# Modulation columns from column chunks of w_mod, summed by TensorE between V's steps

## The chip, the cores and the metric

The kernel runs on one core of one Trainium2 chip. The metric is the device time of one execution in microseconds (us). A core has five engines that run side by side, each working through its own list of instructions in order: TensorE (PE in the profile, with its weight loads shown apart as PEld), VectorE (DVE), ScalarE (ACT), GpSimd (POOL) and SyncE (SP), which here issues the DMAs. [...]

## The reference, cut to what matters

```python
S, D, H = 2048, 448, 16
mod = (silu(c) @ w_mod).reshape(1, 6, 1, D)          # w_mod: 448 x 2688
sa, ca, ga, sb, cb, gb = (mod[:, i] for i in range(6))
h = layernorm(x) * (1 + ca) + sa                     # x: 1 x 2048 x 448
x = x + ga * attention(h)                            # q, k, v = h @ wqkv, 16 heads, softmax, @ wo
h = layernorm(x) * (1 + cb) + sb
x = x + gb * gated_mlp(h)                            # gelu(h @ w_in), a 2048 x 2048 spatial mix, @ w_out
```

Everything is float32. The change lies in the first line and the first use of it: the vectors `sa` and `ca`, and the first h.

## The kernel before, in words

**Stages.** The kernel starts with a short stage that loads x and weights, normalizes and transposes x and computes V, Q and K; attention over 16 heads follows, then the gated MLP. The change touches the start alone, some 50 of 1402 us. There x is worked on in four groups of 512 rows (`g`), each of four tiles of 128 rows. A group's tile is normalized by VectorE (`ln_stat`, `ln_norm`: statistics, then `xn`), transposed by TensorE into four PSUM banks, one for each 128 columns of D (`tp`, c = 0 to 3, the last with 64 real columns), scaled by `1 + ca` and shifted by `sa` (columns, one value to a partition), and split into a high and a low float32r part, `hT`, since products are made of float32r pieces: high by high, high by low, low by high. The weights are split the same way (`wv` for V, `wqk` for Q and K). `STEPS` lists 11 pairs (piece of h, piece of weight); one unit of V (128 rows) or of Q/K (128 features of one group) is 11 products summed in a PSUM bank. Piece 6 holds column block 3, its high part on partitions 0 to 63 and its low part on 64 to 127; the last two pairs, (6,6) and (6,7), read both.

**The modulation before.** `w_mod` is laid out as four row blocks (k) of 112 rows; `load_mod(0)` reads the 896 columns of `sa` and `ca` in four DMAs, one for each k. VectorE multiplies block k by `silu[:, k]` and adds it up over k in `acc` (`mod_acc`, and `mod_last` for the last k, cut into 128-column pieces). A product of TensorE with a column of ones sums over the 112 partitions and turns the row into a column (`pc`, line 380); `mod_cols` copies it to `col_ca` and `col_sa`. Each float32 product stands as two instructions in the trace, each float32r product and each transpose as one.

**The order.** The schedule is written by hand: each engine runs its instructions as the code issues them. PE starts with products whose results nobody reads (`pe_fill`, tile `wu`), which keep it busy until the transposes of group 0 can be made (`tp_first`). Then `mod_last` (line 364 on), `mod_cols`, `h_hi` (ACT: high part of h straight out of PSUM, line 398), `h_full` (DVE: full h, line 393), `h_lo` (full minus high) and `wv_hi`/`wv_lo` follow for each c; `v_mm` makes V of the first four tiles step by step, then `qk_unit((0, 3), 0)` the first Q/K units, `ln_next(1)` transposes group 1, and `qk_unit((1,), 0)` and `qk_unit((2,), 0)` follow. In `ln_transpose` ACT writes the full h (`hfull`, two buffers, line 125) and its high part (line 132), DVE the low part (line 85, the helper `sub`).

**The queues.** SP issues the loads in the order of the code. A DMA's issue can wait for the one eight places before it, and for the buffer it writes: the first Q/K weights ("a", 128x512 pieces) use the buffers of `wm`, the second ("b") those of V's raw weights.

Of the kernel before, what the change touches and what calls it, by code (L numbers as in the profile page):

```python
# [33 lines left out]
def tile_adaln_mha_gmlp(ctx, tc, x, wqkv, wo, w_in, w_spT, b_sp, w_out, cT, w_mod, out):  # L34
# [136 lines left out]
    def load_mod(pair, eng):  # L171
        for k in range(4):
            wms[pair, k] = e1.tile([112, 2, D], F32, name="wm", tag=("wm", "wm", "raw")[pair], bufs=4)
            eng.dma_start(wms[pair, k], w_mod[:, pair, k])
# [44 lines left out]
    def pe_fill(n, with_):  # L219
        for _ in range(n):  # L220
            pe.matmul(wu[:, 0:128], with_[:, 0:128], ones, start=True, stop=True)
# [25 lines left out]
    def ln_stat(g, ts):  # L247
        if g not in mv1:
            mv1[g] = e1.tile([128, 4, 2], F32, name="mv"), e1.tile([128, 4], F32, name="rs")
        for t in ts:  # L250
            st = e1.tile([128, 6], F32, name="st", bufs=4)
            dve.bn_stats(out=st, in_=xts[4 * g + t])
            dve.bn_aggr(out=mv1[g][0][:, t, :], in_=st)

    def ln_rs(g, a, e):
        mv, rs = mv1[g]
        rstd_of(mv[:, a:e, 1], rs[:, a:e], e - a)

    def ln_norm(g, ts):
        mv, rs = mv1[g]  # L260
        for t in ts:
            xn = e1.tile([128, 512], F32, name="xn", bufs=4)
            dve.tensor_scalar(
                out=xn[:, :D],
                in0=xts.pop(4 * g + t),
                scalar1=mv[:, t, 0:1],
                scalar2=rs[:, t : t + 1],
                op0=ALU.subtract,
                op1=ALU.mult,
            )  # L270
            act.activation(xn[:, D:], xn[:, 384:D], AF.Copy)
            xn1.setdefault(g, []).append(xn)

    def v_mm(kts, steps=STEPS, own=None, kind=None):
        pvs = [ps_o.tile([128, 512], F32, name="pv", tag="o") if kt == own else bank("pv", kind) for kt in kts]
        for j, (a, b) in enumerate(steps):
            for kt, pv in zip(kts, pvs):
                g, t = divmod(kt, 4)
                pe.matmul(pv[:, :D], hT[g][:, a, t * 128 : (t + 1) * 128], wv[:, b, :], start=j == 0, stop=j == NST - 1)  # L279
        return list(zip(kts, pvs))  # L280
# [57 lines left out]
    def tp_first(t):  # L338
        for c in range(4):
            pe.transpose(tps[c][:, t * 128 : (t + 1) * 128], xn1[0][t][:, c * 128 : (c + 1) * 128], ident)  # L340

    x1, x3 = xts[1], xts[3]
    ln_stat(0, (0, 1))
    ln_rs(0, 0, 2)
    ln_norm(0, (0, 1))
    ln_stat(0, (2, 3))
    ln_rs(0, 2, 4)
    mod_acc(0, 0)
    mod_acc(0, 1)
    ln_norm(0, (2, 3))  # L350
    mod_acc(0, 2)
    pe_fill(9, x1)
    tp_first(0)
    tp_first(1)
    pe_fill(5, x3)
    tp_first(2)
    tp_first(3)
    pe_fill(4, x3)

    acc0 = [stage.tile([128, 512], F32, name="acc0", tag="qh")[0:112] for _ in range(2)]  # L360
    wm3 = wms.pop((0, 3))

    def mod_last(c):

# [12 lines left out]
        if c == 3:
            pcs[c] = bank("pc", "s")
        for i, part in enumerate((1, 0)):
            pe.matmul(  # L380
                pcs[c][:, i : i + 1], acc0[part][:, c * 128 : (c + 1) * 128], ones[:112, 0:1], start=True, stop=True
            )

    def mod_cols(c):
        for i, (nm, plus1) in enumerate((("ca", 1.0), ("sa", 0.0))):
# [19 lines left out]
        else:  # L405
            sub(eng, hT[0][64:128, 6, :], fs[3][64:128], hT[0][64:128, 6, :])

    for i in (0, 2, 1, 3):
        load_w("a", i, sp)
    wv_hi(0)  # L410
    wv_hi(2)
    mod_last(0)
    pe_fill(1, x3)
    mod_last(2)
    pe_fill(1, x3)
    mod_last(1)
    pe_fill(1, x3)
    mod_cols(0)
    h_hi(0)
    mod_last(3)  # L420
    mod_cols(2)
    h_hi(2)
    mod_cols(1)
    mod_cols(3)
    wv_hi(1)
    h_hi(1)
    wv_hi(3)
    h_hi(3)
    wv_lo(0, dve)
    wv_lo(2, dve)  # L430
    h_full(0)
    h_lo(0, pool)
    h_full(2)
    h_full(1)
    h_full(3)
    wv_lo(3, pool)
    wv_lo(1, dve)
    h_lo(2, dve)
    h_lo(1, dve)
    h_lo(3, dve)  # L440
    load_x(2, sp)
    for i in (0, 2, 1, 3):
        load_w("b", i, sp)
    pvs = v_mm((0, 1, 3, 2), [STEPS[j] for j in (0, 1, 2, 3, 6, 4, 7, 5, 8, 9, 10)], 3, "s")
    qk_part("a", 0, dve)
    qk_part("a", 2, dve)
    ln_stat(1, (0, 1))
    ln_rs(1, 0, 2)
    ln_stat(1, (2, 3))
    ln_norm(1, (0, 1))  # L450
    ln_rs(1, 2, 4)
    qk_part("a", 1, dve)
    qk_part("a", 3, dve)
    load_mod(1, sp)
    for a in pvs:
        v_copy(*a)
    ln_norm(1, (2, 3))
    load_x(3, sp)
    ln_stat(2, range(4))
    turn[0] = 5  # L460
    qk_unit((0, 3), 0)
    ln_rs(2, 0, 4)

    def ln_next(g):
# [6 lines left out]
            ln_norm(g + 1, range(4))  # L471

    ln_next(1)
    qk_unit((1,), 0)
    qk_unit((2,), 0)
    for i in (0, 2, 1, 3):
        qk_part("b", i, dve)
# [892 lines left out]
```

## Time and profile before

| | |
|---|---|
| time, median of 3 runs | 1404.16 us (1404.03 to 1404.17) |
| the profiled execution | 1404.07 us; its span 1401.8 us |
| PE busy in the span | 1390.6 us (99%) |
| DVE, ACT, POOL busy | 1023.5, 769.9, 288.9 us |
| first product of V (line 279) | at 17.70 us |
| first product of Q/K (line 294) | at 27.11 us |
| first transpose of group 1, of group 2 (line 118) | at 33.51, at 44.75 us |

The span runs from the first to the last instruction; 2.3 us of the execution's time lie around it. Times in the text are counted from the span's start. In a row of the timeline the numbers are the start and the length of a run of equal instructions; in a row of the chain of waits the start and the time that the step holds the chain; in a group's row the busy time, the mean of one instruction, the idle time of the engine ahead of it and what ended that.

### The profile page before, as it was taken

Reading aid. Unit: us, or ns where it says so; the run is one execution under the profiler, and the core shown is the slowest. Engines: PE = TensorE matmul, PEld = TensorE weight load, DVE = VectorE, ACT = ScalarE, POOL = GpSimd, SP = SyncE. Lnnn points to the kernel's source line nnn. Section 1 sums busy time; section 2 is a strip of 40 time slices with the busy share of each in tenths; the row PEclk is TensorE's granted clock in tenths of the full one; section 3 lists DMA queues with packets and bytes.
Section 4 is the critical chain, followed back from the end, with each engine's and each line's share of the span. In section 5 each row is a group of like instructions: output and inputs, shape, how many; then the busy total and the mean of one; then the engine's idle time right before and its main releaser. Section 6 shows DMA issues by size and latency. Waiting matters only on the chain.

```text
span 1401.8 us, 20142 instructions
## 1 busy us (share of the span) xinstructions
PE 1390.6 (99%) x7180; PEld 989.5 (71%) x7180; DVE 1023.5 (73%) x1758; ACT 769.9 (55%) x1477; POOL 288.9 (21%) x275
## 2 busy tenths in 40 slices
PE   7999999999999999999999999999999999999998
PEld 7888655555555555555555555988998888888888
DVE  7778888888888888888888860751357655767474
ACT  3723577766667777777666679263234543434211
POOL 2033312222214143313211231100142330000000
PEclk9999999999999999999999999999999999999999
DMA  8564635555555556654434211534103333446453
GB/s 247 166 178 153 193 103 178 167 161 146 166 159 174 156 165 174 186 145 157 129 94 113 63 50 44 188 115 138 54 0 107 112 113 113 142 136 206 144 170 113
DMA packets 102285, 193.42 MB, mean 138 GB/s; under 512 B 17063, under 2 KB 32039, under 8 KB 99639
## 3 DMA queue, kind: packets, MB, share of 16 engines
q1 hardware_dynamic: 99754, 188.30, 44.3%
q10 hardware_dynamic: 2430, 3.84, 0.7%
q8 instruction: 56, 0.92, 0.3%
q14 instruction: 45, 0.36, 0.1%
HBM read 133.63 MB, written 53.67 MB: 134 GB/s over the span
## 4 chain that ended last, share of the span: by engine, by line
PE 98%; DVE 1%; DMA 1%; SPq 0%; issue 0%; ACT 0%; DVEq 0%; ACTq 0%
PE st_ps L581 18%; PE o_ps L596 17%; PE mt L551 17%; PE acc L1148 6%; PE acc L1150 6%; PE acc L1149 6%; PE z_ps L1074 5%; PE z_ps L960 5%; PE pq L294 5%; PE wo_ps L830 3%; PE pv L279 2%; PE y_ps L1250 2%; PE y_ps L1251 2%; PE y_ps L1249 2%; PE tp L118 1%; DMA wm<-in_w_mod_dram 1%
## 5 line engine op out<-in xcount | busy, mean ns | idle before, releaser
L556 DVE TENSOR_REDUCE pm<-mt 128x1 f32<-128x512 f32 x1024 | 631.4, 682 | 84.1 <-PE mt L551 83.5
L585 ACT ACTIVATE P<-st_ps 128x512 f32<-128x512 f32 x1024 | 514.4, 633 | 205.1 <-PE st_ps L581 205.1
L581 PE MATMUL st_ps<-qst,kst 128*128 128x512 f32 x1024 | 404.2, 406 | 0.2 <-DVE qf L300 0.2
L551 PE MATMUL mt<-kst,qst 128*128 128x512 f32 x1024 | 402.9, 393 | 0.1
L581 PEld LDWEIGHTS st_ps<-qst,kst 128*128 128x128 f32 x1024 | 191.3, 188 | 138.0 <-issue 93.9
L596 PE MATMUL o_ps<-P,V 128*32 128x512 f32 x2048 | 247.1, 598 | 0.0
L551 PEld LDWEIGHTS mt<-kst,qst 128*128 128x128 f32 x1024 | 192.4, 188 | 36.2 <-DVE pm L556 3.7
L724 POOL TENSOR_TENSOR ws_raw<-ws_raw 128x512 f32<-128x512 f32 x80 | 102.9, 1287 | 353.1 <-DMA ws_raw<-in_w_spT_dram 352.9
L1036 ACT ACTIVATE wsp_h<-raw_sp 128x512 fp32r<-128x512 f32 x112 | 70.2, 632 | 162.8 <-PE acc L1150 119.0
L85 DVE TENSOR_TENSOR wsp_l<-raw_sp,wsp_h 128x512 fp32r<-128x512 f32 x112 | 80.6, 730 | 90.5 <-ACT wsp_h L1036 89.6
L596 PEld LDWEIGHTS o_ps<-P,V 128*32 128x32 f32 x2048 | 54.7, 109 | 123.0 <-issue 114.7
L1148 PE MATMUL acc<-wsp_h,heapA 128*128 128x512 f32 x224 | 87.3, 390 | 0.0
L1149 PE MATMUL acc<-wsp_l,heapA 128*128 128x512 f32 x224 | 87.2, 389 | 0.0
L1150 PE MATMUL acc<-wsp_h,heapA 128*128 128x512 f32 x224 | 87.2, 389 | 0.0
L1149 PE MATMUL acc<-wsp_l,heapB 128*128 128x512 f32 x174 | 67.7, 389 | 0.0
L1150 PE MATMUL acc<-wsp_h,heapB 128*128 128x512 f32 x174 | 67.7, 389 | 0.0
L1148 PE MATMUL acc<-wsp_h,heapB 128*128 128x512 f32 x174 | 67.7, 389 | 0.0
L294 PE MATMUL pq<-heapD,heapD 128*128 128x512 f32 x196 | 62.6, 392 | 0.8 <-ACT heapD L96 0.8
L1078 DVE BATCH_NORM_STATS2 stz<-z 128x6 f32<-128x448 f32 x32 | 19.9, 625 | 50.4 <-ACT z L1077 29.9
L1148 PEld LDWEIGHTS acc<-wsp_h,heapA 128*128 128x128 f32 x224 | 42.0, 188 | 8.9 <-DVE cD L1154 0.3
L1150 PEld LDWEIGHTS acc<-wsp_h,heapA 128*128 128x128 f32 x224 | 42.0, 188 | 8.8
L1149 PEld LDWEIGHTS acc<-wsp_l,heapA 128*128 128x128 f32 x224 | 42.0, 188 | 8.6
(208 smaller groups left out, 1589.7 us busy)
## 6 DMA issues: line engine op xcount, KB each, us to landing
ws_raw<-in_w_spT_dram SPq DMA_DIRECT2D x160, 256.0 KB
ws_scr<-ws_raw SPq DMA_DIRECT2D x80, 256.0 KB
raw_sp<-ws_scr SPq DMA_DIRECT2D x80, 256.0 KB
kst<-qk_scr SPq DMA_DIRECT2D x45, 224.0 KB
qst<-qk_scr SPq DMA_DIRECT2D x45, 224.0 KB
raw_sp<-in_w_spT_dram SPq DMA_DIRECT2D x32, 256.0 KB
qk_scr<-qh SPq DMA_DIRECT2D x28, 256.0 KB
qk_scr<-ql SPq DMA_DIRECT2D x28, 256.0 KB
```

Of the source, the lines that this page charges most:

```text
L85: eng.tensor_tensor(out=dst, in0=a, in1=hi.bitcast(F32), op=ALU.subtract)
L294: pe.matmul(pq, wqk[:, b, m * 128 : (m + 1) * 128], hT[g][:, a, :], start=j == 0, stop=j == NST - 1)
L551: pe.matmul(mt, qst[h % 3][:, t * 128 : (t + 1) * 128], kst[h % 3][:, kb * 512 : (kb + 1) * 512], start=True, stop=True)
L556: dve.tensor_reduce(out=pms[h][:, t, kb : kb + 1], in_=mt, axis=AX.X, op=ALU.max)
L581: pe.matmul(st, kst[h % 3][:, kt * 128 : (kt + 1) * 128], qst[h % 3][:, qb * 512 : (qb + 1) * 512], start=True, stop=True)
L585: act.activation(p, st, AF.Exp, scale=SCALE)
L596: pe.matmul(otile[h][32 * qb : 32 * qb + 32, :], V[:, kt, h, :], ptiles.pop((u, qb)), start=kt == 0, stop=kt == NT - 1)
L724: pool.tensor_tensor(out=a, in0=a, in1=b, op=SUMS[i // 16][2])
L1036: act.activation(hi, raw, AF.Copy)
L1148: pe.matmul(acc[i], zh, hi, start=st == 0, stop=False)
L1149: pe.matmul(acc[i], zh, lo, start=False, stop=False)
L1150: pe.matmul(acc[i], zl, hi, start=False, stop=st == 7)
```

## The change

- The 896 columns for `ca` and `sa` are read in four chunks by columns, each with all four k (`load_mod_chunk`: 448 KB for c = 0, 1, 2, 224 KB for c = 3), in turn with V's weights, in the order 0, 2, 1, 3. The host lays `w_mod` out so that each chunk is contiguous for a partition.
- `mod_acc`, `mod_last` and their VectorE instructions go for this pair. `mod_sum` makes the columns by TensorE alone: chunk c is the stationary operand, `silu[:, k]` the moving one, four products summed over k in PSUM for each of `ca` and `sa` (for c = 3 twice, 64 columns each, to fill both halves of the partitions).
- `mod_sum(0)` stands ahead of the transposes, `mod_sum(2)` behind them, `mod_sum(1)` and `mod_sum(3)` inside V's products, ahead of the fifth and the seventh step, with the work that needs them (`first_cols`). V's steps are put in the order (0,0) (0,3) (3,0) (2,2) (2,5) (5,2) (1,1) (1,4) (4,1) (6,6) (6,7).
- The filling products: 22 with the identity (there from 1.3 us on), 8 with x, 2 between the transposes, in place of 9, 5, 4 and 3 with x.
- `qk_unit((1,), 0)` moves ahead of the transposes of group 1; V's tiles 4 and 5 are made side by side; group 1's statistics come behind all four Q/K weight parts, its second half's `ln_norm` behind the first Q/K units; x's groups 1 and 2 and the Q/K weights are issued in another order.

```diff
+    def load_mod_chunk(c, eng):
+        n = 128 if c < 3 else 64
+        wms[0, c] = e1.tile([112, 1024], F32, name="wm", tag="wm", bufs=4)[:, : 8 * n].rearrange("p (k a n) -> p k a n", a=2, n=n)
+        eng.dma_start(wms[0, c], w_mod[:, c * 1024 : c * 1024 + 8 * n].rearrange("p (k a n) -> p k a n", a=2, n=n))
...
-    load_mod(0, sp)
     for i in (0, 2, 1, 3):
+        load_mod_chunk(i, sp)
         load_w("v", i, sp)
-    load_x(1, sp)
...
+    def mod_sum(c, kind):
+        if c not in pcs:
+            pcs[c] = bank("pc", kind)
+        w = wms.pop((0, c))
         for i, part in enumerate((1, 0)):
-            pe.matmul(
-                pcs[c][:, i : i + 1], acc0[part][:, c * 128 : (c + 1) * 128], ones[:112, 0:1], start=True, stop=True
-            )
+            for r in (0,) if c < 3 else (0, 64):
+                for k in range(4):
+                    pe.matmul(
+                        pcs[c][r : r + w.shape[-1], i : i + 1], w[:, k, part, :], silu[:, k : k + 1], start=k == 0, stop=k == 3
+                    )
...
+    load_w("a", 0, sp)
+    load_w("a", 2, sp)
+    load_x(1, sp)
+    load_w("a", 1, sp)
+    load_w("a", 3, sp)
+    load_x(2, sp)
+
+    ln_stat(0, (0, 1))
+    ln_rs(0, 0, 2)
+    ln_stat(0, (2, 3))
+    ln_rs(0, 2, 4)
+    ln_norm(0, (0, 1))
+    ln_norm(0, (2, 3))
+    pe_fill(22, ident)
+    pe_fill(8, x1)
+    mod_sum(0, None)
+    tp_first(0)
+    tp_first(1)
+    pe_fill(2, x3)
+    tp_first(2)
+    tp_first(3)
+    mod_sum(2, None)
...
+    def first_cols(c):
+        mod_sum(c, "m")
+        wv_hi(c)
+        mod_cols(c)
+        h_hi(c)
+        h_full(c)
+        wv_lo(c, dve)
+        h_lo(c, dve)
+        if c == 3:
+            for i in (0, 2):
+                qk_part("a", i, dve)
+
+    pvs = v_mm(
+        (0, 1, 3, 2),
+        [STEPS[j] for j in (0, 2, 4, 1, 3, 5, 6, 7, 8, 9, 10)],
+        3,
+        "s",
+        {4: lambda: first_cols(1), 6: lambda: first_cols(3)},
+    )
...
+    turn[0] = 5
+    qk_unit((0, 3), 0)
     ln_norm(1, (2, 3))
     load_x(3, sp)
+    qk_unit((1,), 0)
     ln_stat(2, range(4))
-    turn[0] = 5
-    qk_unit((0, 3), 0)
     ln_rs(2, 0, 4)
...
-        v_tile(4 * g)
-        v_tile(4 * g + 1)
+        if g == 1:
+            for a in v_mm((4, 5)):
+                v_copy(*a)
+        else:
+            v_tile(4 * g)
+            v_tile(4 * g + 1)
```

TensorE's list of instructions from the program's start to V's last product. Before, filling products (`wu`), the transposes (`tp`) and, after VectorE's sums (`acc`), two products with ones for each c (`pc`), then V's 44 products (`pv`) in one piece:

```order
L221 MATMUL wu<-ones,xg 128x128 x9
L340 MATMUL tp<-ident,xn 128x128 x8
L221 MATMUL wu<-ones,xg 128x128 x5
L340 MATMUL tp<-ident,xn 128x128 x8
L221 MATMUL wu<-ones,xg 128x128 x4
L380 MATMUL pc<-ones,acc_227 128x1
L380 MATMUL pc<-ones,acc_226 128x1
```

The same place in the changed program:

```order
L226 MATMUL wu<-ones,ident 128x128 x22
L226 MATMUL wu<-ones,xg 128x128 x8
L358 MATMUL pc<-silu,wm 128x1 x8
L347 MATMUL tp<-ident,xn 128x128 x8
L226 MATMUL wu<-ones,xg 128x128 x2
L347 MATMUL tp<-ident,xn 128x128 x8
L358 MATMUL pc<-silu,wm 128x1 x8
L286 MATMUL pv<-wv,heapD_89 128x448 x16
L358 MATMUL pc<-silu,wm 128x1 x8
L286 MATMUL pv<-wv,heapD_89 128x448 x8
L358 MATMUL pc<-silu,wm 64x1 x16
L286 MATMUL pv<-wv,heapD_89 128x448 x20
```

Eight products with ones (16 instructions) have become 40 products with `silu` (80 instructions), 24 of them inside V's.

VectorE's list around the last of the columns and the splits of h (`heapD_89` from `hfull`), of V's weights (`wv`) and of the Q/K weights (`heapD_91`, `heapF` from `raw`). Before:

```order
L386 TENSOR_SCALAR col_ca<-pc 128x1
L386 TENSOR_SCALAR col_sa<-pc 128x1
L85 TENSOR_TENSOR wv<-raw,wv 128x448 x2
L393 TENSOR_SCALAR hfull<-tp,col_ca,col_sa 128x512 x4
L85 TENSOR_TENSOR wv<-raw,wv 128x448
L85 TENSOR_TENSOR heapD_89<-hfull,heapD_89 128x512 x2
L85 TENSOR_TENSOR heapD_89<-hfull,heapD_89 64x512
L85 TENSOR_TENSOR heapD_91<-raw,heapD_91 128x512
```

In the changed program, for c = 3, the last in turn:

```order
L364 TENSOR_SCALAR col_ca<-pc 128x1
L364 TENSOR_SCALAR col_sa<-pc 128x1
L371 TENSOR_SCALAR hfull<-tp,col_ca,col_sa 128x512
L85 TENSOR_TENSOR wv<-raw,wv 64x448
L85 TENSOR_TENSOR heapD_89<-hfull,heapD_89 64x512
L85 TENSOR_TENSOR heapD_91<-raw,heapD_91 128x512
L85 TENSOR_TENSOR heapF<-raw,heapD_91 128x512 x2
L85 TENSOR_TENSOR heapF<-raw,heapF 64x512
L257 BN_STATS st<-xg 128x6
```

The splits that the last steps of V need, and the four of the Q/K weights, now stand behind columns that TensorE makes in the middle of V; and the two subtractions that POOL did (c = 0's `h_lo`, c = 3's `wv_lo`) are VectorE's. Both readers of a bank `tp` are ordered: `h_full(c)` waits for `h_hi(c)`.

More of the change, by code (lines that the diff above doesn't have):

```diff
@@ L173, in load_mod @@
             wms[pair, k] = e1.tile([112, 2, D], F32, name="wm", tag=("wm", "wm", "raw")[pair], bufs=4)
-            eng.dma_start(wms[pair, k], w_mod[:, pair, k])
+            a = (pair * 4 + k) * 2 * D
+            eng.dma_start(wms[pair, k], w_mod[:, a : a + 2 * D].rearrange("p (a b) -> p a b", b=D))
+    def load_mod_chunk(c, eng):
+        n = 128 if c < 3 else 64
+        wms[0, c] = e1.tile([112, 1024], F32, name="wm", tag="wm", bufs=4)[:, : 8 * n].rearrange("p (k a n) -> p k a n", a=2, n=n)
+        eng.dma_start(wms[0, c], w_mod[:, c * 1024 : c * 1024 + 8 * n].rearrange("p (k a n) -> p k a n", a=2, n=n))
     def load_x(g, eng):
@@ L272, in ln_norm, with v_mm @@
             xn1.setdefault(g, []).append(xn)
-    def v_mm(kts, steps=STEPS, own=None, kind=None):
+    def v_mm(kts, steps=STEPS, own=None, kind=None, mid=None):
         pvs = [ps_o.tile([128, 512], F32, name="pv", tag="o") if kt == own else bank("pv", kind) for kt in kts]
         for j, (a, b) in enumerate(steps):
+            if mid and j in mid:
+                mid[j]()
             for kt, pv in zip(kts, pvs):
@@ L406, in h_lo @@
             sub(eng, hT[0][64:128, 6, :], fs[3][64:128], hT[0][64:128, 6, :])
-    for i in (0, 2, 1, 3):
-        load_w("a", i, sp)
-    wv_hi(0)
[L411 to L417, printed above, removed]
+    load_w("a", 0, sp)
[19 more added lines that the diff above has]
+    mod_sum(2, None)
+    wv_hi(0)
     mod_cols(0)
     h_hi(0)
-    mod_last(3)
+    wv_lo(0, dve)
+    h_full(0)
     mod_cols(2)
+    h_lo(0, dve)
+    wv_hi(2)
     h_hi(2)
[L423 to L429, printed above, removed]
-    wv_lo(2, dve)
[L431 to L437, printed above, removed]
-    h_lo(2, dve)
-    h_lo(1, dve)
-    h_lo(3, dve)
-    load_x(2, sp)
+    h_full(2)
+    wv_lo(2, dve)
+    h_lo(2, dve)
+    def first_cols(c):
[16 more added lines that the diff above has]
+    )
+    for i in (1, 3):
+        qk_part("a", i, dve)
     for i in (0, 2, 1, 3):
         load_w("b", i, sp)
-    pvs = v_mm((0, 1, 3, 2), [STEPS[j] for j in (0, 1, 2, 3, 6, 4, 7, 5, 8, 9, 10)], 3, "s")
-    qk_part("a", 0, dve)
-    qk_part("a", 2, dve)
+    load_mod(1, sp)
+    for a in pvs:
+        v_copy(*a)
     ln_stat(1, (0, 1))
@@ L473, in tile_adaln_mha_gmlp @@
     ln_next(1)
-    qk_unit((1,), 0)
     qk_unit((2,), 0)
@@ L507, in tile_adaln_mha_gmlp @@
             load_head(0, 1536, S)
-        v_tile(4 * g)
-        v_tile(4 * g + 1)
+        if g == 1:
+            for a in v_mm((4, 5)):
+                v_copy(*a)
+        else:
+            v_tile(4 * g)
+            v_tile(4 * g + 1)
         if g == 3:
@@ L1345 @@
     from concourse.bass_utils import run_bass_kernel_spmd as _run
+    wm = _np.asarray(inputs["w_mod"]).reshape(4, 112, 3, 2, 448).transpose(1, 2, 0, 3, 4)
+    w_mod = _np.concatenate(
+        [wm[:, 0, :, :, c : c + 128].reshape(112, -1) for c in (0, 128, 256, 384)] + [wm[:, 1:].reshape(112, -1)], axis=1
+    )
     lay = {
@@ L1355 @@
         "cT": inputs["c"].reshape(4, 112).T,
-        "w_mod": _np.asarray(inputs["w_mod"]).reshape(4, 112, 3, 2, 448).transpose(1, 2, 0, 3, 4),
+        "w_mod": w_mod,
     }
```

38 lines of the change are left out of this document (removed).

## The prediction

> **What bounds the kernel now.** I read the page first, then PE's waits, then the chain of waits and the timeline of the first 70 us.
>
> ```profile
> PE 98%; DVE 1%; DMA 1%; SPq 0%; issue 0%; ACT 0%; DVEq 0%; ACTq 0%
> PE wu L221 <- DVE st L252: 4.9, 1, 4.9
> PE tp L340 <- DVE xn L263: 1.3, 1, 1.3
> PE pq L294 <- ACT heapD L96: 0.8, 1, 0.8
> PE st_ps L581 <- DVE qf L300: 0.2, 1, 0.2
> ```
>
> PE is the chain for 98% of the span, and the four rows of its waits are all: after the Q/K wait at 31 us it stands still for 0.2 us in 1370. So whatever moves PE's list at some 50 us moves the end by as much; nothing later can take it up. The question is when PE ends group 2's transposes (46.42 us), behind which both programs list the same products: 44 of V, 44 of Q/K, 32 transposes and 22 more of V stand ahead of that in each.
>
> ```profile
> 4.94 4.18 PE L221 MATMUL wu<-ones,xg 128*128 128x128 f32 x18 [4.94 <-DVE st L252]
> 8.91 1.91 PE L340 MATMUL tp<-ident,xn 128*128 128x128 f32 x8
> 10.62 1.39 PE L221 MATMUL wu<-ones,xg 128*128 128x128 f32 x10
> 17.70 9.57 PE L279 MATMUL pv<-wv,heapD 128*128 128x448 f32 x44
> 27.11 1.52 PE L294 MATMUL pq<-heapD,heapD 128*128 128x512 f32 x6
> 33.51 1.91 PE L118 MATMUL tp<-ident,xn 128*128 128x128 f32 x16
> 44.75 1.91 PE L118 MATMUL tp<-ident,xn 128*128 128x128 f32 x16
> 46.42 4.73 PE L279 MATMUL pv<-wv,heapD 128*128 128x448 f32 x22
> ```
>
> ```profile
> 14.42 0.89 PE wu L221 x8
> 15.83 0.33 PE wu L221 x2
> ...
> 17.50 0.35 PE pc L380 x4
> ...
> 33.67 1.75 PE tp L118 x16
> 35.41 5.02 PE pq L294 x22
> 40.43 4.48 PE pv L279 x22
> ```
>
> The chain gives PE's price for one instruction with no wait in it: 0.204 us for V (4.48/22), 0.228 for Q/K (5.02/22), 0.109 for a transpose, 0.111 for a filling one (0.89/8). By these V's 44 need 8.96 us, while the starts 17.70 and 27.11 leave 9.41: 0.45 of waits. The first 22 of Q/K need 5.0 and have 6.40 (27.11 to 33.51): 1.4 of waits. Those 1.85 us and an earlier start of V are all that there is to win.
>
> **Price of a column sum.** Twelve `pc` instructions and six filling ones lie between 15.83 and 17.85 (17.50 + 0.35): 2.02/18 = 0.112 us each, so a product of one column costs as much as one of 128; its weight load sets the pace. For 64 columns:
>
> ```profile
> 65.21 0.94 PE L237 MATMUL pc<-ones,acc 112*128 112x1 f32 x10
> 66.08 2.51 PE L279 MATMUL pv<-wv,heapD 128*128 128x448 f32 x11
> ```
>
> The ten (six of 128 columns, four of 64) take 0.87 until V goes on; less 6 x 0.112 that leaves 0.05 for each of 64. Eight float32 products are 16 instructions, so `mod_sum` of c = 0, 1, 2 costs 16 x 0.112 = 1.8 us, that of c = 3 32 x 0.05 = 1.6. Bounds: 0.112 for 64 columns too (3.6), and below nothing but the product itself.
>
> **Start of V.** PE can begin when the identity is made, at 1.3.
>
> ```profile
> 1.00 0.29 POOL masks.py:199 TENSOR_SCALAR_AFFINE_SELECT ident<-ident 128x128 f32<-128x128 f32 x1
> 8.63 0.63 DVE L252 BATCH_NORM_STATS2 st<-xg 128x6 f32<-128x448 f32 x1 [0.66 <-DMA xg<-in_x_dram]
> 11.69 1.15 DVE L232 SCALAR_TENSOR_TENSOR acc<-wm,silu,acc 112x896 f32<-112x896 f32 x1 [0.90 <-DMA wm<-in_w_mod_dram]
> 12.76 0.93 DVE L263 TENSOR_SCALAR xn<-xg,mv,rs 128x448 f32<-128x448 f32 x2
> ```
>
> PE starts slow: the first 18 products take 4.18/18 = 0.232 us, the transposes behind them 0.24; only within the next ten, at about 10.8, does the price fall to 0.11. That is 5.9 us after the first. Counted from 1.35 the fast clock comes at 7.2, and 25 of the 60 filling instructions are slow; the other 35 end at 7.2 + 35 x 0.111 = 11.1. Then `mod_sum(0)` 1.8, eight transposes 0.87, four fillings 0.44, eight transposes 0.87, `mod_sum(2)` 1.8: V starts at 16.9, **0.8 earlier** than 17.70. The covers hold: x's last piece lands at 8.6 and w_mod's second DMA at 11.6 (392 KB each, two in 3.0 us), so the 448 KB of chunk 0 are there at 10.3 and, behind V's 224 KB, chunk 2 at 13; the last two `xn`, behind L232's 1.15 us before, end no later than the 13.7 of before, and PE asks for them at 14.2. VectorE's sums of w_mod go, but they win only what PE's own list ahead of V lets through.
>
> [...]
>
> The rows give these bounds: no earlier than chunk 0 (V at 16.1), no later than a fast clock at 10.8 as before (12.9 for the fillings, V at 18.7).
>
> **Inside V.** 8.96 for V, 1.8 and 1.6 for the sums: 12.4 us. And a new wait. The sum of c = 3 ends after 24 products of V, at 16.9 + 4.9 + 3.4 = 25.2. Steps (6,6) and (6,7) need `h_lo(3)`, and between stand in a row:
>
> ```profile
> L386 DVE TENSOR_SCALAR col_ca<-pc 128x1 f32<-128x1 f32 x4 | 0.6, 154 | 0.4 <-PE pc L380 0.4
> L398 ACT ACTIVATE heapD<-tp,col_sa,col_ca 128x512 fp32r<-128x512 f32 x4 | 3.0, 769 | 0.0
> L393 DVE TENSOR_SCALAR hfull<-tp,col_ca,col_sa 128x512 f32<-128x512 f32 x4 | 3.0, 803 | 0.0
> L85 DVE TENSOR_TENSOR wv<-raw,wv 128x448 fp32r<-128x448 f32 x3 | 2.1, 712 | 0.0
> L85 DVE TENSOR_TENSOR heapD<-hfull,heapD 64x512 fp32r<-64x512 f32 x4 | 2.8, 690 | 2.0 <-ACT heapD L132 1.9
> L380 PE MATMUL pc<-ones,acc 112*128 112x1 f32 x16 | 2.2, 237 | 0.0
> ```
>
> 0.2 until the sum is out, 0.25 for the two columns, 0.77 `h_hi`, 0.8 `h_full`, 0.6 `wv_lo`, 0.7 `h_lo`: 3.3 us, to 28.55. PE has three steps between (12 x 0.204 = 2.4, to 27.65) and waits 0.9. V ends at 28.55 + 1.63 = 30.2, 3.1 later than 27.11.
>
> **Behind V.** The first Q/K units run without a wait: chunk 3 frees the buffer of the last "a" weight at 25.2, and such a DMA of 256 KB needs 1.2 us behind another (20.80 to 21.98 below), so it is there before VectorE, whose four low parts (0.65 each, from 28.6) end at 31.2; the first step that reads the third is due at 33. So 5.0 instead of 6.4: they end at 35.2, 1.7 later than 33.51. But now VectorE comes late with everything behind:
>
> ```profile
> 20.80 0.63 ACT L96 ACTIVATE heapD<-raw 128x512 fp32r<-128x512 f32 x1 [0.37 <-DMA raw<-in_wqkv_dram]
> 21.98 0.63 ACT L96 ACTIVATE heapD<-raw 128x512 fp32r<-128x512 f32 x1 [0.54 <-DMA raw<-in_wqkv_dram]
> ...
> L252 DVE BATCH_NORM_STATS2 st<-xg 128x6 f32<-128x448 f32 x16 | 9.6, 603 | 0.9 <-DMA xg<-in_x_dram 0.9
> L253 DVE BATCH_NORM_AGGREGATE mv<-st 128x2 f32<-128x6 f32 x16 | 2.9, 182 | 0.5
> L263 DVE TENSOR_SCALAR xn<-xg,mv,rs 128x448 f32<-128x448 f32 x16 | 7.3, 507 | 1.2 <-POOL rs L109 1.2
> L85 DVE TENSOR_TENSOR heapD<-hfull,heapD 128x512 fp32r<-128x512 f32 x11 | 7.3, 684 | 4.8 <-ACT heapD L132 4.8
> L309 ACT ACTIVATE qh<-pq 128x512 fp32r<-128x512 f32 x10 | 5.6, 596 | 7.9 <-PE pq L294 7.9
> L125 ACT ACTIVATE hfull<-tp,col_sa,col_ca 128x512 f32<-128x512 f32 x12 | 9.2, 771 | 1.5 <-DVE heapD L85 1.5
> L132 ACT ACTIVATE heapD<-hfull 128x512 fp32r<-128x512 f32 x12 | 7.6, 632 | 0.4
> ```
>
> - Group 1's transposes. From 31.2: statistics of four tiles 4 x 0.785 = 3.1, two `xn` 0.9, to 35.2; the two Q/K splits wait for ACT's `qh` (36.0) and end at 37.3; two more `xn` at 37.8 and 38.2. PE ends `qk_unit(1)` at 37.7 and needs the fourth `xn` after three transposes, at 38.0: it waits **0.3**, then 39.8.
> - V of tiles 4 and 5. PE ends `qk_unit(2)` at 42.3. VectorE has split unit 1 by 39.8, does group 2's statistics until 42.9, then the low parts of c = 0 and 2 (44.2). ACT's third `hfull` waits for one of two buffers, freed at 43.6: then 0.77 and 0.63 for each of c = 1 and 3, their low parts at 45.8 and 47.2. V's steps, two products each, reach (1,1) at 44.8 (wait 0.3) and (6,6) at 46.4 (wait 0.8, and some 0.1 for each restart): **1.3** in all, end 48.1.
> - Group 2's transposes. Four `xn` from 47.2 on, the last at 49.0; PE gets to it at 48.4: **0.7**, end 50.5.
>
> **The sum**, against 46.42: start -0.8; sums in V +3.4; V's waits 0.9 for 0.45, +0.45; Q/K's -1.4; then +0.3, +1.3, +0.7. That is +3.95, and 50.5 - 46.42 = 4.1 by the times; I take 4.0. The profiled execution took 1404.07 (2.3 around its span), 0.09 below the median, so the forecast is **1408.1 us**. With the clock's bounds, +3.2 to +5.8. With c = 3 at 3.6, +6.0. If none of the four new waits comes (0.9 + 0.3 + 1.3 + 0.7 = 3.2), +0.8.
>
> **Rivals.**
> 1. VectorE keeps up and the new waits stay out. For it: VectorE had idle time there before (the 1.9 and 4.8 us of its `heapD` rows). Against: its list of 3 us behind h_lo(3) and two subtractions more, which POOL did. +0.8 to +2.7: 1405 to 1406.8.
> 2. The other side: **weight loads vanish behind other products**, and the column sums cost next to nothing. V would start when `h_hi(0)` is ready (transposes over at 14.0, then 0.8: 14.9, 2.0 earlier) and hold no 3.4: 4.0 - 5.4 = -1.4, 1402.7; without the new waits 1399.5. It decides below half of the price: the four sums come to 7.0 us, and at 3.0 the change breaks even. Against it stand the 0.87 us at 65.21, taken between V's products. [...]
> 3. The fillings with the identity don't bring the fast clock earlier than 10.8: +5.8, 1409.9. Against: it came 5.9 us after the first product.
> 4. A sum by TensorE alone that still waits for VectorE: excluded, its operands are DMAs' data and `silu`, which VectorE makes ahead of its first statistics.
>
> **How the numbers follow.** Forecast 0.64, rival 1 0.19, rival 2 0.09, rival 3 0.08. A measurement tells 0.2%, 2.8 us, from no change. Slower by more: the forecast but for early clocks with a missing wait, and rival 3: 0.70. Within: rival 1, half of rival 2, the rest: 0.25. Faster: 0.05. The range, 1405.0 to 1409.3, holds the forecast and rival 1 and leaves out rival 2, rival 3 and the dearest c = 3.
>
> **What would show it.** In the changed profile: V's first product at 16 to 17.5, Q/K's first at 30, group 1's transposes at 37.7, group 2's over at 50.5; PE waits for VectorE in V's last eight products, at line 118 and in tiles 4 and 5; 16 `pc` instructions in 1.8 us. A first Q/K product before 28 would make it wrong (sums cheap, or h_lo(3) early), and so would PE without waits from 36 to 50.

## The result: 0.5% slower, and the place where the time was lost

| | before | after |
|---|---|---|
| median of six runs each, us | 1404.1 (1403.64 to 1404.28) | 1411.44 (1411.01 to 1412.21) |
| the profiled execution, us | 1404.07, span 1401.8 | 1411.14, span 1409.1 |
| V's first product on TensorE, us | 17.70 | 15.62 |
| group 2's transposes over, us | 46.42 | 53.28 |

The ratio of the times is 1.0053, with an interval of 1.004 to 1.0066. The forecast was 1408.1 with a range up to 1409.3: the direction came out, the size did not.

Of the profile after, first the shares of the chain that ended last, by engine, from the page:

```profile
PE 98%; DVE 1%; DMA 0%; ACT 0%; issue 0%; POOL 0%; POOLq 0%; DVEq 0%; ACTq 0%
```

TensorE is the chain as before. All but the last of its waits, 0.2 us, again lie in the first 55 us (engine, line, what it waited for; us in total, times, the longest):

```profile
PE pv L286 <- DVE heapD L85: 2.5, 3, 1.2
PE pv L286 <- ACT heapD L132: 2.1, 3, 1.5
PE wu L226 <- POOL ident masks.py:199: 1.3, 1, 1.3
PE st_ps L580 <- DVE qf L307: 0.2, 1, 0.2
```

The wait of 4.9 us for x's first statistics has gone with the products of the identity, and the waits of the first transposes and of Q/K have gone too. New are 4.6 us at line 286, which is V. The timeline of TensorE says where in V (start, length, line, what, how many):

```profile
1.34 7.02 PE L226 MATMUL wu<-ones,ident 128*128 128x128 f32 x44 [1.34 <-POOL ident masks.py:199]
...
15.62 3.51 PE L286 MATMUL pv<-wv,heapD 128*128 128x448 f32 x16
18.97 1.84 PE L358 MATMUL pc<-silu,wm 112*128 112x1 f32 x16
20.67 1.86 PE L286 MATMUL pv<-wv,heapD 128*128 128x448 f32 x8
22.47 1.41 PE L358 MATMUL pc<-silu,wm 112*64 112x1 f32 x32
23.80 2.72 PE L286 MATMUL pv<-wv,heapD 128*128 128x448 f32 x12
27.24 1.87 PE L286 MATMUL pv<-wv,heapD 128*128 128x448 f32 x8 [0.72 <-DVE heapD L85]
28.95 1.52 PE L301 MATMUL pq<-heapD,heapD 128*128 128x512 f32 x6
...
36.44 1.94 PE L118 MATMUL tp<-ident,xn 128*128 128x128 f32 x16
...
42.41 0.98 PE L286 MATMUL pv<-wv,heapD 128*128 128x448 f32 x2 [1.51 <-ACT heapD L132]
...
46.43 1.27 PE L286 MATMUL pv<-wv,heapD 128*128 128x448 f32 x4 [1.19 <-DVE heapD L85]
...
50.88 2.54 PE L118 MATMUL tp<-ident,xn 128*128 128x128 f32 x16
53.28 4.75 PE L286 MATMUL pv<-wv,heapD 128*128 128x448 f32 x22
```

Up to 36.44 the plan held, and better than forecast. Then, behind the Q/K unit of m = 2 (40.74 by the rows left out), V of tiles 4 and 5 takes until 50.88: 10.1 us for 22 products that took 4.5 before. Each term of the forecast's ledger, read in the two timelines as the distance from one start to the next:

| term | forecast | measured |
|---|---|---|
| start of V | -0.8 | -2.08 (17.70 to 15.62) |
| V up to the first Q/K product: sums and waits | +3.85 | +3.92 (13.33 for 9.41) |
| first 22 Q/K products | -1.4 | -1.41 (4.99 for 6.40) |
| group 1's transposes | +0.3 | +0.03 (1.69 for 1.66) |
| V of tiles 4 and 5 | +1.3 | **+5.66** (10.14 for 4.48) |
| group 2's transposes | +0.7 | +0.73 (2.40 for 1.67) |
| group 2's transposes over | +4.0 | +6.86 |

The spans differ by 7.3 us; the last 0.4 arise later and are looked at below.

What held V of tiles 4 and 5 stands in the chain of waits of after (start, us, what):

```profile
33.91 0.61 ACT qh L316
...
34.54 0.72 DVE ql L85 x2
35.26 6.78 DMA qk_scr<-ql
...
42.17 0.69 DVE ql L85
...
46.41 0.79 ACT hfull L125
...
49.22 0.70 DVE heapD L85
...
49.94 1.80 DVE xn L268 x4
```

A store is on the chain: `qk_scr<-ql`, which takes 6.78 us. VectorE has the first low part `ql` done at about 35.2, its store is issued at 35.26, and what follows is the `ql` of the third Q/K unit, 7 us later. The low part has two buffers (as `qh` has), and the third unit needs the first one's again, which is free when its store has landed. VectorE's timeline shows the wait as its own:

```profile
42.17 0.69 DVE L85 TENSOR_TENSOR ql<-pq,qh 128x512 fp32r<-128x512 f32 x1 [5.49 <-DMA qk_scr<-ql]
```

and ScalarE's, 1.7 us earlier, for the high part:

```profile
40.43 0.60 ACT L316 ACTIVATE qh<-pq 128x512 fp32r<-128x512 f32 x1 [3.40 <-DMA qk_scr<-qh]
```

Behind the first wait stand group 2's statistics and then the low parts of group 1's h; behind the second, group 1's full h. V of tiles 4 and 5 needs both. In before this unit's split stands behind group 1's h on both engines (ScalarE at 43.18) and finds its buffers free.

Why the store took that long, in SyncE's issues (in order of time):

```profile
25.11 0.54 SPq L185 DMA_DIRECT2D xg<-in_x_dram  x1
...
28.37 2.42 SPq L175 DMA_DIRECT2D wm<-in_w_mod_dram  x4
34.54 0.35 SPq L322 DMA_DIRECT2D qk_scr<-qh  x1
```

Ahead of it went 896 KB of x, 768 KB of the "b" weights and 4 x 392 KB of w_mod, 3.2 MB in 5.7 us, at a time when about 0.3 MB move in a us (329 and 305 GB/s in the windows below). In before the same loads went out between 18.3 and 32.4 us, and from 30 to 32 us, ahead of the stores, the DMA share there was 0.12. The windows of after show the engines of the DMA full from 26 us on (length, busy time and count for each engine, granted clock, DMA share, GB/s):

```profile
24.00:26.00 2.00, 2.00 (x11) 1.84 (x11) 1.09 (x4) 1.77 (x4) 0.00 (x0) 1.00 0.29 81
26.00:30.00 4.00, 3.28 (x16) 2.64 (x15) 3.94 (x7) 2.67 (x7) 0.00 (x0) 1.00 0.98 329
...
34.00:38.00 4.00, 4.00 (x27) 3.47 (x26) 2.13 (x4) 1.51 (x4) 0.00 (x0) 1.00 1.02 305
38.00:42.00 4.00, 2.89 (x15) 2.10 (x13) 0.00 (x0) 1.54 (x3) 0.00 (x0) 1.00 1.10 223
```

VectorE did nothing at all from 38 to 42. That is a reading of one trace; whether the buffer and the loads ahead of the store are the cause was then tried.

### The profile page after: what moved, and what is told of

Same layout as the page of the kernel before. It is cut to its first block, busy times and chain, and to the rows that moved or that the text cites. A ratio compares the mean times of both kernels' runs of the same rounds, so it can differ in the third digit from the quotient of the medians.

```text
span 1409.1 us, 20301 instructions
## 1 busy us (share of the span) xinstructions
PE 1398.9 (99%) x7266; PEld 995.0 (71%) x7266; DVE 1020.2 (72%) x1749; ACT 770.7 (55%) x1477; POOL 289.6 (21%) x273
## 4 chain that ended last, share of the span: by engine, by line
PE 98%; DVE 1%; DMA 0%; ACT 0%; issue 0%; POOL 0%; POOLq 0%; DVEq 0%; ACTq 0%
PE st_ps L580 18%; PE o_ps L595 17%; PE mt L550 17%; PE acc L1149 6%; PE acc L1147 6%; PE acc L1148 6%; PE z_ps L1073 5%; PE z_ps L959 5%; PE pq L301 4%; PE wo_ps L829 3%; PE pv L286 2%; PE y_ps L1249 2%; PE y_ps L1248 2%; PE y_ps L1250 2%; PE tp L118 1%; PE wu L226 1%
```

## The experiments

The theory: the third Q/K unit, moved ahead of group 1's transposes, waits for a buffer whose store is queued behind loads; that wait is the 4.4 us by which V of tiles 4 and 5 exceeds its forecast (5.66 for 1.3), and the rest of the ledger stands. The rival: VectorE's and ScalarE's lists themselves are too long there, and the store only hides it. The median of before beside each group of runs was 1404.1 (e1 to e4), 1404.51 (e5 to e8) and 1403.77 us (e9, e10). The ratios are those on record and differ from the quotients of the medians by up to 0.0006. Since single executions of one kernel scatter by some us (before's own from 1402.25 to 1407.42), the times of TensorE within the trace are read with them.

| run | time, us | ratio to before, interval | V starts | group 2's transposes over |
|---|---|---|---|---|
| after | 1411.44 | 1.0053, 1.004 to 1.0066 | 15.62 | 53.28 |
| e1 own buffers | 1407.62 | 1.0024, 1.0014 to 1.0033 | 16.08 | 49.16 |
| e2 unit behind | 1410.03 | 1.0036, 1.0026 to 1.0046 | 16.1 | 51.47 |
| e3 w_mod late | 1408.57 | 1.0029, 1.002 to 1.0039 | 16.01 | 49.76 |
| e4 no identity | 1415.57 | 1.0081, 1.0064 to 1.0098 | 19.57 | 56.95 |
| e5 two by VectorE | 1406.28 | 1.0019, 1.0009 to 1.0028 | 16.63 | 49.12 |
| e6 statistics early | 1406.42 | 1.001, 1.0001 to 1.0019 | 16.27 | 48.58 |
| e7 five and six | 1405.41 | 1.0005, 0.9996 to 1.0015 | 16.19 | 47.66 |
| e8 before, identity | 1404.02 | 0.9998, 0.9988 to 1.0007 | 17.02 | 45.70 |
| e9 ScalarE's full h | 1403.97 | 1.0002, 0.9993 to 1.001 | 16.75 | 46.77 |
| e10 before, Q/K weights first | 1402.85 | 0.9993, 0.9984 to 1.0002 | 17.55 | 45.19 |

**e1: the third unit's own buffers.** Its parts go to two pieces of `hT[3]`, which group 3 fills much later; the loads stay where they are.

```diff
-            hi = stage.tile([128, 512], F32R, name="qh")
-            lo = stage2.tile([128, 512], F32R, name="ql")
+            hi = hT[3][:, 0, :] if own else stage.tile([128, 512], F32R, name="qh")
+            lo = hT[3][:, 1, :] if own else stage2.tile([128, 512], F32R, name="ql")
...
-    qk_unit((1,), 0)
+    qk_unit((1,), 0, own=True)
```

> The split of the third Q/K unit (m = 1) gets a pair of buffers of its own, in a part of hT that is not yet in use; the order of all instructions stays. Theory 1 (the two qh/ql buffers, freed only when the first units' stores have landed behind 3.25 MB of loads, hold ACT until 40.4 and VectorE until 42.2): ACT starts that unit's high part near 37 instead of 40.4, group 2's transposes end about 4 us earlier (near 49.3 instead of 53.3), time 1407.3 us (1406.6 to 1408.0). Theory 2 (VectorE's own list is late as forecast, the store wait only fills its slack): less than 1 us gained, 1410.5 to 1411.6.

TensorE's timeline in e1 from the first of tiles 4 and 5 on:

```profile
41.24 4.04 PE L286 MATMUL pv<-wv,heapD 128*128 128x448 f32 x18
...
46.76 2.54 PE L118 MATMUL tp<-ident,xn 128*128 128x128 f32 x16
49.16 4.75 PE L286 MATMUL pv<-wv,heapD 128*128 128x448 f32 x22
```

Tiles 4 and 5 take 5.52 us (41.24 to 46.76): 1.04 more than before, where the forecast had 1.3. The ledger of e1 is -1.62 (V starts at 16.08), +3.92, -1.37, +0.03, +1.04 and +0.73, in sum +2.74, and its span is 2.7 us longer than before's. The buffer is worth 4.6 us of the 10.14. The theory holds, and of the remaining forecast every term but V's start (-1.62 for -0.8) comes out within 0.3.

**e3: the loads behind the stores.** The buffers stay two; w_mod's second half and x's group 3 are issued behind the third unit's stores.

```diff
-    load_mod(1, sp)
...
-    load_x(3, sp)
     qk_unit((1,), 0)
+    load_x(3, sp)
+    load_mod(1, sp)
```

> The four loads of w_mod for the second pair (1.6 MB) and x's group 3 are issued behind the third unit's stores instead of ahead of the first unit's. Theory 1: only x's group 2 and the second Q/K weights (1.7 MB) stand ahead of the stores, which land near 37 (qh) and 39 (ql): VectorE's third split starts at 38 to 39.5 instead of 42.2, time 1407.3 to 1408.5. Theory 2: no change, 1410.5 to 1412.

ScalarE's `qh` of the third unit comes at 37.49 without a wait. In e3's chain of waits the store on it takes 2.81 us instead of 6.78, and VectorE's `ql` waits 1.52 us, as its timeline shows below:

```profile
35.71 2.81 DMA qk_scr<-ql
```

```profile
38.64 0.69 DVE L85 TENSOR_TENSOR ql<-pq,qh 128x512 fp32r<-128x512 f32 x1 [1.52 <-DMA qk_scr<-ql]
```

Tiles 4 and 5 take 6.17 us; the median, 1408.57, lies 0.07 above the expected range. Two edits that share nothing, more buffers and fewer bytes ahead, take away 4.6 and 4.0 of the same 5.66 us: the wait needs both the missing buffer and the queue.

**e2: the third unit back behind group 1's transposes**, where before has it, with the rest as changed.

```diff
-    qk_unit((1,), 0)
     ln_stat(2, range(4))
...
     ln_next(1)
+    qk_unit((1,), 0)
     qk_unit((2,), 0)
```

> The third Q/K unit goes back behind group 1's transposes, where it stood before the change; the rest of the change stays. Theory 1: its wait for the stores no longer stands ahead of ACT's full h and VectorE's statistics, but PE now waits some 2 us for group 1's last two normalized tiles (ready near 36.3, asked for at 33.9); about 1407 us (1406.3 to 1408). Theory 2: the time stays within 1 us of 1411.4, or grows by the wait at the transposes (to 1413).

The time came out 3 us above the 1407 that the theory gave it, and 1.4 below after, which is not the rival's either. The waits in tiles 4 and 5 are gone altogether (45.32 to 49.80, 4.48 us as in before, and 1.67 for group 2's transposes). But a new one stands ahead of them, and something else with it. TensorE's timeline of e2:

```profile
36.79 2.32 PE L118 MATMUL tp<-ident,xn 128*128 128x128 f32 x14 [1.98 <-DVE xn L268]
38.77 1.63 PE L301 MATMUL pq<-heapD,heapD 128*128 128x512 f32 x3
```

Without the unit there is nothing to do while VectorE makes the second half of group 1's `xn`: TensorE waits 1.98 us, and the transposes take 4.34 us with it for 1.69. Then four Q/K products go from 38.77 to 40.62, 0.46 us each for the usual 0.228, and the 22 of both units take 6.55 for 5.11. The windows of e2 show what went with it (the granted clock is the third number from the right):

```profile
36.50:39.00 2.50, 2.12 (x15) 1.93 (x16) 2.43 (x7) 1.91 (x5) 0.00 (x0) 0.89 1.04 259
39.00:41.00 2.00, 2.00 (x6) 1.56 (x6) 1.93 (x6) 1.62 (x4) 0.74 (x2) 0.50 1.08 284
41.00:43.00 2.00, 2.00 (x8) 1.60 (x7) 0.96 (x2) 1.94 (x4) 1.17 (x1) 0.79 1.03 317
```

Some 1.7 us after the wait the granted clock was halved (0.50 from 39 to 41), by estimate for some 3.4 us (reckoned with 1.00 and 0.50 alone, a mean of 0.89 over 2.5 us is 0.55 us at half, then 2.0, and 0.79 over 2 us is 0.84): the Q/K products lost 1.44 us by it, besides the wait. It seems not to come in every execution: of e2's eight, three have a granted clock of 1.000 over the whole span and took 1406.85 to 1408.37 us, near the expected 1407; the five others, at 0.998 or 0.999, took 1409.98 to 1411.29. Only the profiled one, of the five, has a trace. So moving the unit ahead was right for the gap; what it lacked was a buffer.

**e4: the products of the identity left out.** It asks what they are worth in the changed order.

```diff
-    pe_fill(22, ident)
     pe_fill(8, x1)
```

> The 22 filling products with the identity are left out; PE starts with x at about 4.9 us. If the fast clock comes 3.8 us after the first product (as the changed kernel's 44 instructions in 6.9 us suggest), it is there at 8.7, before the first chunk's sum, and V starts at most 0.4 later: 1411.4 to 1412. If it comes 5.9 us after (as forecast), sum and transposes run slow until 10.8 and V starts 0.8 to 1.5 later: 1412.2 to 1413.

1415.57, above the 1413 expected at most: both alternatives left out that TensorE could be slow again behind a wait. TensorE's timeline of e4:

```profile
4.62 3.43 PE L226 MATMUL wu<-ones,xg 128*128 128x128 f32 x16 [4.62 <-DVE st L257]
10.57 3.17 PE L358 MATMUL pc<-silu,wm 112*128 112x1 f32 x16 [2.52 <-DMA wm<-in_w_mod_dram]
```

The eight products with x end at 8.0, slow ones all (0.21 us an instruction, at a granted clock of 1.00), TensorE stands still for 2.52 us until chunk 0 has come at 10.5, and is slow again behind that: the sum takes 3.0 us for 1.7, the transposes 0.22 us each. The windows from 10.5 to 18 us in e4, with the granted clock third from the right:

```profile
10.50:14.00 3.50, 3.43 (x18) 3.46 (x19) 1.15 (x5) 1.08 (x4) 0.38 (x1) 0.57 1.06 211
14.00:18.00 4.00, 4.00 (x22) 4.00 (x21) 0.54 (x2) 0.49 (x1) 0.00 (x0) 0.52 1.01 215
```

V starts 3.95 us later than in after. Here the products of the identity buy 4 us; what they buy in before's order is e8.

**e5: the columns of c = 1 and 3 from VectorE's sums again** (on e1), so that only 12 products with ones stand inside V; c = 0's low part and c = 3's of the weights go to POOL as before, and c = 3 comes one step later.

```diff
+    def mod_dve(c):
+        w = wms.pop((0, c))
...
+        dve.tensor_scalar(out=acc, in0=w[:, 0], scalar1=silu[:, 0:1], scalar2=None, op0=ALU.mult)
+        for k in range(1, 4):
+            dve.scalar_tensor_tensor(out=acc, in0=w[:, k], scalar=silu[:, k : k + 1], in1=acc, op0=ALU.mult, op1=ALU.add)
...
-    h_lo(0, dve)
+    h_lo(0, pool)
+    mod_dve(1)
...
+    wv_lo(3, pool)
...
-        {4: lambda: first_cols(1), 6: lambda: first_cols(3)},
+        {4: lambda: first_cols(1), 7: lambda: first_cols(3)},
```

> On top of the run with own buffers: the columns of c = 1 and 3 are summed over k by VectorE again (four instructions each, between V's steps), with one product with ones for each column; the low parts of h's c = 0 and of V's weight c = 3 go back to POOL; c = 3's product stands ahead of V's eighth step. If the column sums inside V cost PE what the forecast took (3.4 us, 3.0 in the changed kernel's rows), V's 44 products with what lies between take 11.0 to 11.6 us instead of 13.3, and the time falls by 1.8 to 2.3 against the run with own buffers: 1405.3 to 1405.9. Rival: VectorE, with these sums back, holds V's last steps as much as PE's sums did: less than 0.8 gained, 1406.8 to 1407.7.

1406.28 lies between the two expected ranges, and the trace decides for the rival. By the medians e5 lies 1.3 us below e1, by the ratios 0.7 (the two ran in different rounds); in the trace V takes 12.76 us (16.63 to 29.39) for 13.33, 0.6 us less where 1.8 to 2.3 were expected: the sums inside it fell from 3.03 to about 0.7, and 2.05 us of waits for VectorE came in their place (0.58 and 0.86 for `wv`, 0.36 for `acc`, 0.25 for `heapD`). The edit also puts c = 1's low parts, of the weights and of h, behind c = 3's columns (lines not shown above); the wait of 0.86 stands there.

**e6: the statistics of one tile of group 2 ahead of the first Q/K units** (on e1).

```diff
     ln_rs(1, 2, 4)
+    ln_stat(2, (0,))
...
-    ln_stat(2, range(4))
+    ln_stat(2, (1, 2, 3))
```

> On top of the run with own buffers: the statistics of group 2's first tile stand ahead of the first Q/K units, where VectorE waits 1.1 us for ACT. The forecast's account of tiles 4 and 5 (0.6 us at V's last step) and of group 2's transposes (0.7) hangs on VectorE's list being 0.8 too long there: both waits shrink by 0.5 to 0.8, 1.0 to 1.4 us gained, 1406.2 to 1406.7. Rival: these waits come from ACT's four full h, not from VectorE: less than 0.4 gained.

1406.42, inside the expected range; in the trace only the first of the two waits went. Tiles 4 and 5 go from 41.41 to 46.18 without a wait, 4.77 us; group 2's transposes stay at 2.40, since their `xn` still come last of VectorE's list. That is 0.75 us for an expected 1.0 to 1.4, and more than the rival's 0.4. So e1's remaining 1.04 us there were the length of VectorE's list, as the forecast had it, and 0.75 of them can be had by its order.

**e7: e5 and e6 together.**

> The last two edits together on top of the run with own buffers. If they add: 2.8 to 3.7 us below it, 1403.9 to 1404.9, about the time before. If both only move the same VectorE list: no better than the better of the two alone, 1405.3 to 1405.9.

1405.41, half a us above the expected end and inside the rival's range. The trace speaks for the sum: from V's start to the end of group 2's transposes e7 takes 31.47 us, for 33.08 in e1, 32.49 in e5 and 32.31 in e6, so e7 gains 1.6 us where its parts gain 0.6 and 0.8. V's waits for `wv` are still there, 0.90 and 0.86. POOL's and then VectorE's timeline of e7, ahead of the first of the two, show why:

```profile
16.06 1.30 POOL L85 TENSOR_TENSOR heapD<-hfull,heapD 128x512 fp32r<-128x512 f32 x1 [4.88 <-DVE hfull L388]
...
19.27 1.14 POOL L85 TENSOR_TENSOR wv<-raw,wv 64x448 fp32r<-64x448 f32 x1 [1.91 <-ACT wv L330]
...
16.50 1.01 DVE L366 TENSOR_SCALAR acc<-wm,silu 112x256 f32<-112x256 f32 x1
...
19.71 1.17 DVE L85 TENSOR_TENSOR wv<-raw,wv 128x448 fp32r<-128x448 f32 x1
```

A VectorE instruction of 256 columns takes 1.01 us while POOL subtracts and ends 0.15 us behind POOL's; the subtraction for which TensorE waits takes 1.17 us beside POOL's second one, 0.61 or 0.62 in after, where POOL does nothing from 12 to 29 us. The second wait, 0.86, is not POOL's: VectorE makes that `wv` behind c = 3's columns, at 24.16. In e9, where POOL does nothing there, the instruction of 256 columns takes 0.35:

```profile
17.73 0.35 DVE L366 TENSOR_SCALAR acc<-wm,silu 112x256 f32<-112x256 f32 x1
```

The two rows put the price of the instruction of 256 columns at 0.66 us beside POOL's subtraction; what in the two engines makes it, no row shows.

**e9: on e7, ScalarE makes the full h of c = 1, 2 and 3**, VectorE takes POOL's two subtractions back, and the low parts of the weights come ahead of the columns that are not there yet.

```diff
+        if eng is act:
+            act.activation(fs[c], tps[c], AF.Identity, scale=cols["ca"][:, c : c + 1], bias=cols["sa"][:, c : c + 1])
+            return
...
-    h_lo(0, pool)
-    mod_dve(1)
     wv_hi(2)
-    h_hi(2)
-    h_full(2)
     wv_lo(2, dve)
+    mod_cols(2)
+    h_lo(0, dve)
+    h_hi(2)
+    h_full(2, act)
+    mod_dve(1)
...
-    wv_lo(3, pool)
```

> On top of e7: ACT, not VectorE, makes the full h of c = 1, 2 and 3; the low part of V's weight c = 2 comes ahead of its columns; POOL's two subtractions are VectorE's again. If the 2.0 us of waits inside V in e7 are VectorE's list there, made longer by POOL's work at the same time (the first 256-column instruction took 1.00 us beside POOL's 1.30, the subtraction of V's weight 1.17 instead of 0.61), V's 44 products fall from 12.4 to 10.2 to 11.0 us and group 2's transposes end at 45.3 to 46.5 (47.7 in e7), 1403 to 1404.3, at or below the time before. Without POOL beside it the 256-column instruction takes 0.4 to 0.5 us. Rival: the chain sum, column, high, full and low part of c = 3 holds V whoever does it: less than 0.7 gained.

V takes 11.03 us (16.75 to 27.78) with one wait of 0.59, and group 2's transposes are over at 46.77, 0.35 behind before. V lies 0.03 us above its expected range and the transposes' end 0.27, the time, 1403.97, inside. Ratio 1.0002: the changed order, mended in four places, is as fast as the kernel it replaced, and not faster.

**e8 and e10: parts of the change in the kernel before.** e8 puts the products of the identity ahead of before's filling ones; e10 besides lets VectorE split all of the "a" weights ahead of group 1's statistics, which is the changed program's order.

```diff
+    pe_fill(22, ident)
     pe_fill(9, x1)
...
     qk_part("a", 2, dve)
+    qk_part("a", 1, dve)
+    qk_part("a", 3, dve)
     ln_stat(1, (0, 1))
...
-    qk_part("a", 1, dve)
-    qk_part("a", 3, dve)
```

> The kernel before with 22 filling products of the identity put ahead of its own: its clock is fast by 5 to 6 us instead of 10.8, its transposes take 0.11 instead of 0.24 us. The reading that VectorE's sums of w_mod and the loads, not PE, set V's start there: V at 17.5 to 17.8 as before, time 1403.8 to 1404.4. If the slow start of PE held it: V up to 1 us earlier, 1403.

> The kernel before with the identity's fillings (as e8) and the splits of the last two first Q/K weights moved ahead of group 1's statistics; no column sum by TensorE. The forecast put 1.4 us of the change's gain on those Q/K waits alone. If they come from that order, the first 22 Q/K products take 5.0 to 5.2 us instead of 6.4 and group 2's transposes end 1.0 to 1.4 earlier than in e8 (45.7): 1402.6 to 1403.2. Rival: the wait moves to group 1's transposes, whose normalized tiles come later: less than 0.4 gained, 1403.6 to 1404.2.

e8 is not told apart from before (0.9998): TensorE is at the fast price from about 5 us on (an estimate: 44 filling instructions took 6.80 us, at 0.232 us for a slow and 0.111 for a fast one) and then waits 0.24 us for the third `xn`, which stands on VectorE's list behind the sum of w_mod's second row block, and that waits for its load. In this execution the load came some 0.8 us earlier (the sum began at 10.93 for 11.69), and V started at 17.02. In e10 the first 22 Q/K products have no wait left. TensorE's timeline of e10:

```profile
26.95 1.54 PE L294 MATMUL pq<-heapD,heapD 128*128 128x512 f32 x6
...
31.96 2.20 PE L118 MATMUL tp<-ident,xn 128*128 128x128 f32 x16
```

5.01 us for 6.40; group 1's transposes give 0.3 of it back (1.96 for 1.66). Counted from V's start, group 2's transposes are over after 27.64 us, in before after 28.72: 1.1 us won. The median is the lowest of all, 0.9 us below before's, but its ratio of 0.9993 has an interval up to 1.0002, so it is not shown to be faster.

## Why the forecast fell short, step by step

- **The step that failed** is "V of tiles 4 and 5": "VectorE has split unit 1 by 39.8, does group 2's statistics until 42.9", and so 1.3 us. VectorE split that unit at 42.17 to 42.86 and ended the statistics at 45.8; the term measured 5.66. The step let the splits follow ScalarE's `qh` and asked for no room to write them. The two buffers of `hfull` were counted in it, the two of `qh` and `ql` were not, though three units now stood where two had; and the store that frees them was not followed into SyncE's queue, where the change had put 3.2 MB shortly ahead of it. With the room given (e1) the term is 1.04, with the queue cleared (e3) 1.69.
- **Start of V, a size**: -2.08 for -0.8, below the earliest that the prediction allowed (15.62 for 16.1). Fillings, first sum, transposes and second sum came in the order and at the prices forecast (the 16 instructions of a sum 1.70 for 1.8), but the fast price came earlier. 44 filling instructions went from 1.34 to 8.20, 6.86 us; with 0.232 us for a slow and 0.111 for a fast one some 16 were slow, and the fast price came, by this estimate, 3.8 us after the first, not 5.9. (The granted clock reads 1.00 all through this start, in the window from 1.3 to 5.0 with 17 instructions in 3.7 us as in the next with 29 in 3.2. That a clock makes the slow price, as the forecast's "fast clock" has it, these rows do not show.) Chunk 0 was there by 9.99 for the 10.3 forecast; in e2, e7 and e4 TensorE waited for it until 10.38, 10.47 and 10.57. That both came early in the traced execution took 1.3 us off the total. The other runs with this start (e1 to e3, e5 to e7, e9) begin V between 16.01 and 16.75, all ahead of the forecast's 16.9: the size was off, and that after was the earliest of all is luck. The 5.9 was no slip of before's trace: e5, with after's instructions up to there, has this row in its timeline of TensorE

```profile
1.35 8.02 PE L226 MATMUL wu<-ones,ident 128*128 128x128 f32 x44 [1.35 <-POOL ident masks.py:199]
```

  and e7 this one:

```profile
1.35 6.65 PE L226 MATMUL wu<-ones,ident 128*128 128x128 f32 x44 [1.35 <-POOL ident masks.py:199]
```

  By the same reckoning the fast price came 5.7 and 3.1 us after the first product, and 2.9 in e2; what sets the moment, these runs do not show. The term is one with a spread of more than a us from one execution to the next, and that belongs in a range.
- **Sums in V and V's waits**: +3.92 for +3.85. The sum of c = 1 took 1.70, that of c = 3 1.33 (32 instructions of 0.042, forecast 0.05), the wait for `h_lo(3)` 0.72 for 0.9. What is left, some 0.6, lies in V's own 44 products, which took 9.58 in four pieces for the 8.96 that the prediction worked out for one; what of it is the pieces' edges was not separated.
- **First Q/K products**: -1.41 for -1.4; **group 2's transposes**: +0.73 for +0.7. Right, and the reasons with them: no wait at Q/K, and transposes at the pace of VectorE's `xn`.
- **Group 1's transposes**: 0.03 for 0.3. VectorE's fourth `xn` came at 36.7, in time.
- **Rivals.** That VectorE keeps up (1) is wrong: with the buffer given (e1), waits of 0.71 and 0.57 and the slower transposes stay. That weight loads vanish and the sums cost next to nothing (2) is wrong: 0.106 us for each instruction with one column, two to a product. That the weight load sets this price fits after's rows: with 64 columns of weights in place of 128 the same column cost 0.042, and the 16 loads of a sum stand in PEld's row without a gap, 1.87 us. That the fast price comes no earlier than 10.8 (3) is wrong, by an estimated 5.7 us (5.1 in after). The sums by TensorE wait for no sum of VectorE (4), as said.
- **The last 0.4 us** between 6.86 at 53.28 and 7.3 at the end are open. The attention is where they arise: line 580's first product comes 6.8 us later than before's (159.6 for 152.8), its last 7.4 (876.3 for 868.9). The same difference, what the span lost against before beyond what group 2's transposes had lost, is 0.0 in e1, 0.3 in e3 and 1.3 in e2; it was not followed further.

## What to carry to other kernels

When a step is moved ahead, count the buffers that its outputs rotate through at the new place, and for each one follow what frees it to its end: a store is not over when it is issued, and in a queue shared with loads it can land late by what was issued ahead of it (here 6.78 us after its issue, and 2.81 with 1.6 MB of loads taken out of its way). A product of one column cost TensorE here as much as one of 128, both with 128 columns of weights (0.106 to 0.111 us an instruction; the four sums 6.4 us, 1.70 three times and 1.33), so moving a sum there pays only where the other engine's sum is really what is waited for. Filling products are worth their place only if what follows them on TensorE is not waiting for another engine anyway: the same 22 were worth 4 us in one order (V's start in e4 and after) and nothing that can be measured in the other (e8, 0.9998).

## What the runs showed of the hardware beyond what was expected

- Behind a wait of 1.98 us in group 1's transposes (e2) the granted clock fell to 0.50 for an estimated 3.4 us, beginning 1.7 us after the wait's end (means of 0.89, 0.50 and 0.79 in the windows from 36.5 to 43); behind one of 2.52 us (e4) it stood at 0.50 from about 11 to 17.8 us, by the same estimate (means of 0.57 from 10.5 to 14 and 0.52 from 14 to 18). After's waits of up to 1.5 us in tiles 4 and 5, with products between them, left it at 1.00 (every window from 36 to 56). What in a wait decides it, these runs do not separate.
- The fast price of an instruction (0.111 us for 0.232) came, by the estimate above, between 2.9 (e2) and 5.7 us (e5) after the first product, in executions with the same instructions up to there.
- VectorE's instruction of 256 columns took 1.01 us beside a subtraction on POOL and 0.35 without (e7, e9).
- A 256 KB store behind 3.2 MB of loads took 6.78 us from its issue to its landing (after), and 2.81 with 1.6 MB less ahead of it (e3).
